# w2's rows 8 to 10 loaded in four DMAs of 112, 6, 6 and 4 partitions

## Chip, cores and metric

The kernel runs on one core of a Trainium2 chip. The metric is the time of one execution in microseconds (us), the median over several runs. A profiled execution adds a trace with the time of every instruction and DMA packet. Engines are named as in the profile: PE is TensorE, PEld its weight load, DVE VectorE, ACT ScalarE, POOL GpSimd, SP SyncE (which issues the loads). A trailing q (SPq, PEldq) means the engine's sequencer.

## The reference

One decode step of a transformer block for two tokens, with modulation computed from a condition `c`. All arrays are float32.

```
mod = silu(c) @ w_mod                    # six vectors of 512 per token
h   = layernorm(x) * (1 + ca) + sa
x   = x + ga * attention(h, k_cache, v_cache, wq, wo)
                                         # 32 query heads, 8 key heads of 128,
                                         # the last 4096 positions of the cache
h   = layernorm(x) * (1 + cb) + sb
x   = x + gb * (silu(h @ w1) @ w2)       # w1 512 x 1792, w2 1792 x 512
```

## The kernel before

Nearly all of the work is loading: the caches' last 4096 positions and the weights are 97.5 MB, and each byte is used once for two tokens.

All loads but the one of `c` go through SP's queue into `slots`, a ring of eight slots of 16 KB in each of the 128 partitions. `stream(n)` (line 70) hands out the next `n` slots. A load into a slot waits until the instructions that read its former contents are done. In the order of issue the queue carries `w_mod`, `x`, `wq`, then per step one K load and one V load of 4 MB (`load_pair`, line 77; eight steps), then `wo` in two loads, `w1` in two, and `w2` in four. Each of these loads covers all 128 partitions; a partition's piece lies in one run in memory. Sixteen DMA engines share each of them.

`load_runs(w, per, lo, hi)` (line 88) loads a weight matrix. It gives partition `p` the rows `p * per + lo` to `p * per + hi - 1`. For `w2` `per` is 14 (`T2`), and the four loads (lines 593 to 598) are rows 0 to 7, 8 to 10, 11 and 12, and 13 of each partition: 2048, 768, 512 and 256 KB, or 16384, 6144, 4096 and 2048 B for each partition.

The attention runs in eight steps: VectorE transposes K (line 367), TensorE forms scores (L380), ScalarE the exponentials, TensorE the weighted V (L454). After it, the tail, in the order of TensorE, which is written out by hand (`inorder`):

- L584, the product with `wo`, and the second layernorm
- L623, the product with `w1`, then VectorE's silu, which gives `uT` (L653)
- L657: w2's rows 0 to 7, each one matmul of 512 columns into `acc_yw`, in two passes each (16 in the profile)
- L667: w2's rows 8 to 10, four matmuls of 128 columns each into `acc_y` (24 in the profile)
- `gather` (line 563): ScalarE copies `acc_yw` in two halves (L567), and TensorE adds it to `acc_y` (L571)
- L682: w2's rows 11 to 13 into `acc_l`, in halves of 64 columns (48 in the profile)
- VectorE L690 to L698: times `gb`, plus `x`; then SP stores the output (L700)

The matmuls of L667 read tile rows through `w2t[tt]`, so each waits for the load that brought row `tt`. The `busy` matmuls (L554) between the stages write a scratch bank that nothing reads.

Of the kernel before, what the change touches and what calls it, by code (L numbers as in the profile page):

```python
# [13 lines left out]
P = 128  # L14
# [9 lines left out]
def adaln_block(  # L24
# [19 lines left out]
    nc = tc.nc  # L44
# [25 lines left out]
    def stream(n=1):  # L70
        i = turn_of[0]
        if n % 2 == 0:
            i += -i % n
        turn_of[0] = i + n
        return slots[:, i % RING : i % RING + n, :].rearrange("p s e -> p (s e)")
# [9 lines left out]
        )  # L85
        return t

    def load_runs(w, per, lo, hi):

        e = w.shape[1]  # L90
        n = -(-(hi - lo) * e // 4096)
        t = stream(n)[:, : (hi - lo) * e].rearrange("p (q e) -> p q e", e=e)
        nc.sync.dma_start(t, w.rearrange("(p q) e -> p q e", q=per)[:, lo:hi, :])
        return t


# [2 lines left out]
    x_sp, c_sp = xc[:, 0, :], xc[:, 1, :]  # L99
    nc.vector.memset(xc, 0.0)  # L100
    wm = load_runs(w_mod, 4, 0, 4)
    rows8 = lambda t: t.rearrange("(ab r) m -> ab r m", r=16)[:, 0, :]
    for b in range(B):
        for lo in (0, 2):
# [3 lines left out]
            )  # L108
    nc.sync.dma_start(rows8(x_sp), x2.rearrange("b (g m) -> g b m", m=P))  # L109
    wqt = load_runs(wq, 4, 0, 4)  # L110


# [157 lines left out]
    for k in range(4):  # L270
        ab = wm[:, k, : 2 * D].rearrange("p (s g m) -> p g s m", s=2, g=4)
        cd = wm[:, k, 2 * D :].rearrange("p (s g m) -> p g s m", s=4, g=4)
        for g in range(4):
            r = slice(32 * g, 32 * g + 32)
            nc.tensor.matmul(m_a[r, :], scT[:, k, :], ab[:, g], start=(k == 0), stop=(k == 3))  # L275
        for g in range(4):
            r = slice(32 * g, 32 * g + 32)
# [230 lines left out]
    for lo, hi in ((0, 24), (24, 32)):  # L508
        wt = load_runs(wo, 32, lo, hi)
        wot.extend(wt[:, q, :] for q in range(hi - lo))  # L510
    xT = turned(x_sp, "xT")
    w1t = []
    for lo, hi in ((0, 3), (3, 4)):
        wt = load_runs(w1, 4, lo, hi)
# [78 lines left out]
    T2, WIDE = F // P, 8  # L593
    w2t = {}
    for lo, hi in ((0, WIDE), (WIDE, 11), (11, 13), (13, T2)):
        wt = load_runs(w2, T2, lo, hi)
        for tt in range(lo, hi):
            w2t[tt] = wt[:, tt - lo, :]
    aoT = once.tile([P, 4, 32], F32, tag="zp", name="aoT")
# [78 lines left out]
    for tt in range(11, T2):  # L678
        for h in range(2):
            for g in range(4):  # L680
                lo = g * P + h * H
# [11 lines left out]
    for h in range(2):  # L693
        r = slice(h * H, (h + 1) * H)
        inorder(nc.vector.tensor_mul(yo[:, r], yl[h], gb[:, r]))
    for h in range(2):
        r = slice(h * H, (h + 1) * H)
# [30 lines left out]
```

## Time and profile before

| what | value |
|---|---|
| median of 3 runs | 236.15 us (235.47 to 236.29) |
| the profiled execution's own time | 235.3 us |
| its span, first to last instruction | 233.6 us |
| loads in it | 97.53 MB, 418 GB/s over the span |
| TensorE matmul busy | 163.9 us, 70% |
| VectorE busy | 115.2 us, 49% |
| mean granted TensorE clock | 0.925 |

How to read the rows that follow: a row of the chain of waits is start, length, and the work that released what comes next. A row of the timeline is start, length, engine, line, operation, output and inputs with their shapes, the number of instructions, and in brackets the idle time before them and what ended it. A row of stretches gives the busy time of PE, PEld, DVE, ACT and POOL with their numbers of instructions, the granted clock, the DMA engines' mean busy share, and GB/s. A DMA answer counts packets and how many of them are small. A packet is counted in the stretch in which it starts, so shares of short stretches scatter around 1.

### The profile page before, as it was taken

How to read it: one execution, taken by the hardware profiler on the slowest of the kernel's cores; microseconds unless marked ns; L12 is line 12 of the kernel's file. 1: busy time of each engine (PE TensorE's matmuls, PEld its weight loads, DVE VectorE, ACT ScalarE, POOL GpSimd, SP SyncE). 2: the span in 40 equal slices, each digit the busy share in tenths (PEclk: the TensorE clock that was granted, in tenths of full speed). 3: DMA queues.
4: the chain of work that ended last, by engine and by line, in shares of the span. 5: the costliest groups of instructions: out<-in, count | busy, mean ns of one | idle time of the engine just before them, and what ended most of it. 6: DMA issues, size and time to landing. Idle time of an engine off the chain costs nothing.

```text
span 233.6 us, 2452 instructions
## 1 busy us (share of the span) xinstructions
PE 163.9 (70%) x998; PEld 41.1 (18%) x998; DVE 115.2 (49%) x180; ACT 33.5 (14%) x90; POOL 10.1 (4%) x34
## 2 busy tenths in 40 slices
PE   0004906959697839797598769748759786799984
PEld 0001401301111111211110201201111122233322
DVE  0007230187894758695197189259559540200332
ACT  2000210000311120130310201111030041000321
POOL 3004610000000000000000000000000000000000
PEclk9999995999859985999979979999997999899999
DMA  7998998999999999999999999999999999989991
GB/s 269 438 551 359 404 494 359 446 445 415 410 432 449 446 443 404 421 438 446 449 438 404 426 431 449 449 421 410 424 449 449 443 424 438 466 356 438 423 409 63
DMA packets 3794, 97.68 MB, mean 418 GB/s; under 512 B 432, under 2 KB 456, under 8 KB 968
## 3 DMA queue, kind: packets, MB, share of 16 engines
q1 hardware_dynamic: 3768, 97.53, 97.2%
q8 instruction: 8, 0.13, 0.2%
q14 instruction: 2, 0.02, 0.0%
q10 hardware_dynamic: 16, 0.00, 0.0%
HBM read 97.53 MB, written 0.00 MB: 418 GB/s over the span
## 4 chain that ended last, share of the span: by engine, by line
DMA 61%; issue 17%; DVE 13%; PE 6%; POOL 0%; SPq 0%; POOLq 0%; ACT 0%; DVEq 0%
DMA slots<-in_A_k_cache_dram 22%; DMA slots<-in_A_wq_dram 15%; DMA slots<-in_B_w_dram 12%; DMA slots<-in_A_v_cache_dram 12%; DVE kT L367 11%; PE q L308 3%; PE o L454 2%; DVE zp L426 1%; PE acc_yw L657 1%; DVE xp L424 1%; PE acc_l L682 0%; PE acc_y L667 0%; DVE qT L321 0%; POOL qg L325 0%; SPq L109 0%
## 5 line engine op out<-in xcount | busy, mean ns | idle before, releaser
L367 DVE STREAM_TRANSPOSE kT<-slots 128x1024 f32<-128x1024 f32 x64 | 73.7, 1211 | 22.7 <-DMA slots<-in_A_k_cache_dram 22.6
L380 PE MATMUL s<-kT,qbd 128*32 128x512 f32 x256 | 68.5, 714 | 17.6 <-DVE kT L367 16.6
L454 PE MATMUL o<-slots,ptb 128*32 128x512 f32 x256 | 29.1, 595 | 1.1 <-DMA slots<-in_A_v_cache_dram 1.1
L380 PEld LDWEIGHTS s<-kT,qbd 128*32 128x32 f32 x256 | 9.8, 115 | 69.1 <-DVE kT L367 65.1
L275 PE MATMUL m_a<-slots,scT 128*32 128x256 f32 x32 | 4.4, 500 | 20.6 <-DVE scT L267 20.6
L308 PE MATMUL q<-slots,hq_T 128*32 128x512 f32 x64 | 9.3, 745 | 7.7 <-DMA slots<-in_A_wq_dram 7.7
L554 PE MATMUL junk<-quad,id 128*32 128x512 f32 x24 | 12.9, 672 | 0.0
L466 ACT ACTIVATE ob<-o,own 128x128 f32<-128x128 f32 x32 | 9.1, 368 | 23.9 <-PE o L454 23.9
L410 ACT COPY bias<-bp 128x1 f32<-128x1 f32 x8 | 1.3, 159 | 75.3 <-PE bp L408 75.3
L454 PEld LDWEIGHTS o<-slots,ptb 128*32 128x32 f32 x256 | 7.7, 109 | 16.3 <-issue 16.2
L390 DVE TENSOR_REDUCE mx<-s 128x1 f32<-128x512 f32 x8 | 5.5, 692 | 9.6 <-PE s L380 9.6
L441 ACT ACTIVATE ptb<-pT,odd 128x256 f32<-128x256 f32 x16 | 6.7, 477 | 23.1 <-PE pT L433 23.1
L474 PE MATMUL o_all<-ob,selh 128*64 128x512 f32 x16 | 8.7, 622 | 2.0 <-ACT ob L466 2.0
L426 DVE TENSOR_TENSOR zp<-xp,quarter 128x1024 f32<-128x1024 f32 x8 | 9.8, 1226 | 0.2
L261 DVE STREAM_TRANSPOSE cT<-xc 128x128 f32<-128x128 f32 x1 | 0.4, 402 | 16.8 <-DMA xc<-in_c_dram 16.8
L321 DVE STREAM_TRANSPOSE qT<-q 128x512 f32<-128x512 f32 x2 | 1.4, 716 | 13.8 <-PE q L308 11.9
L433 PE MATMUL pT<-zp,mix 128*32 128x256 f32 x64 | 5.9, 446 | 2.8 <-DVE zp L426 2.3
L584 PE MATMUL acc_o<-slots,oTn 128*32 128x512 f32 x64 | 7.7, 593 | 0.0
L600 DVE STREAM_TRANSPOSE aoT<-ao 128x128 f32<-128x128 f32 x1 | 0.3, 316 | 14.8 <-PE ao L571 14.8
L392 PE MATMUL mT<-ident,mx 128*1 128x128 f32 x16 | 3.0, 271 | 6.4 <-DVE mx L390 6.4
L424 DVE STREAM_TRANSPOSE xp<-pr 128x512 f32<-128x512 f32 x8 | 5.5, 685 | 3.4 <-ACT pr L412 3.4
L278 PE MATMUL m_sp<-slots,scT 128*32 128x512 f32 x32 | 6.6, 712 | 0.0
(138 smaller groups left out, 90.1 us busy)
## 6 DMA issues: line engine op xcount, KB each, us to landing
slots<-in_A_k_cache_dram SPq DMA_DIRECT2D x8, 4096.0 KB, 27.6
slots<-in_A_v_cache_dram SPq DMA_DIRECT2D x8, 4096.0 KB, 27.8
slots<-in_w_mod_dram SPq DMA_DIRECT2D x1, 6144.0 KB, 17.0
slots<-in_A_wo_dram SPq DMA_DIRECT2D x1, 6144.0 KB
slots<-in_B_w_dram SPq DMA_DIRECT2D x1, 2688.0 KB
slots<-in_A_wo_dram SPq DMA_DIRECT2D x1, 2048.0 KB, 29.5
slots<-in_B_w_dram SPq DMA_DIRECT2D x1, 2048.0 KB
slots<-in_B_w_dram SPq DMA_DIRECT2D x1, 896.0 KB
```

The lines of the kernel that those rows point to most:

```text
L278: nc.tensor.matmul(m_sp[r, :], scT[:, k, :], cd[:, g], start=(k == 0), stop=(k == 3))
L308: nc.tensor.matmul(q_ps[n][32 * g : 32 * g + 32, :], hq_T[:, k, :], wv[:, n, g], start=(k == 0), stop=(k == 3),)
L367: inorder(nc.vector.transpose(kT[s, j][:, 32 * c : 32 * c + 32, :], kt[s].rearrange("p (n j r) -> p j n r", j=4, r=32)[:, j, 32 * c : 32 * ...
L380: inorder(nc.tensor.matmul(s_ps[s][r : r + 32, :], qbd[h // 4][:, h % 4, b, j, :], kT[s, j][:, 32 * c : 32 * c + 32, e:32:2], start=(j == ...
L424: inorder(nc.vector.transpose(xp, pr[s]))
L426: inorder(nc.vector.tensor_mul(zp, xp[:, None, :, 0:16].to_broadcast([P, 4, 16, 16]), quarter[:, :, None, None].to_broadcast([P, 4, 16, 16 ...
L441: inorder(nc.scalar.activation(ptb[s % 2][:, :, e, :], tp.rearrange("p (w z) -> p w z", z=16), AF.Copy, scale=odd[:, e : e + 1],))
L454: inorder(nc.tensor.matmul(o_ps[s][r : r + 32, :], ptb[s % 2][:, w].rearrange("p e z -> p (e z)"), vt[s].rearrange("p (c w m f d) -> p c f ...
L466: inorder(nc.scalar.activation(o_sb[s][:, c], o_ps[s][:, c], AF.Copy, scale=own[:, m : m + 1]))
L474: inorder(nc.tensor.matmul(o_all, selh[:, lo : lo + 2 * HQ], o_sb[s], start=(s == 0), stop=(s == STEPS - 1)))
L554: inorder(nc.tensor.matmul(junk[0:32, :], id4, quad.rearrange("p m y -> p (m y)"), start=True, stop=True,))
L584: inorder(nc.tensor.matmul(acc[32 * g : 32 * g + 32, :], oTn[:, q, :], wot[q], start=(q < 4), stop=(q >= 28),))
```

## The change

`load_runs` gets an argument `parts`, the numbers of partitions of consecutive DMAs, with one DMA of 128 as its default. Only the load of w2's rows 8 to 10 uses it: 112 partitions (0 to 111), then 6 (112 to 117), 6 (118 to 123) and 4 (124 to 127). The bytes, their places in `slots`, and the instructions that read them stay the same. SP issues three DMAs more.

```
-    def load_runs(w, per, lo, hi):
+    def load_runs(w, per, lo, hi, parts=(P,)):
 ...
         t = stream(n)[:, : (hi - lo) * e].rearrange("p (q e) -> p q e", e=e)
-        nc.sync.dma_start(t, w.rearrange("(p q) e -> p q e", q=per)[:, lo:hi, :])
+        src, at = w.rearrange("(p q) e -> p q e", q=per)[:, lo:hi, :], 0
+        for rows in parts:
+            r = slice(at, at + rows)
+            nc.sync.dma_start(t[r], src[r])
+            at += rows
+        assert at == P
         return t
 ...
     for lo, hi in ((0, WIDE), (WIDE, 11), (11, 13), (13, T2)):
-        wt = load_runs(w2, T2, lo, hi)
+        wt = load_runs(w2, T2, lo, hi, (112, 6, 6, 4) if lo == WIDE else (P,))
```

## The prediction

> **What bounds the kernel now.** I read the page first, then the chain of waits, then TensorE's timeline, then the DMA answers in narrow windows, because the edited load is one of the last four and only the tail can change.
>
> ```profile
> span 233.6 us, 2452 instructions
> ...
> DMA packets 3794, 97.68 MB, mean 418 GB/s; under 512 B 432, under 2 KB 456, under 8 KB 968
> ...
> q1 hardware_dynamic: 3768, 97.53, 97.2%
> q8 instruction: 8, 0.13, 0.2%
> ...
> q10 hardware_dynamic: 16, 0.00, 0.0%
> ```
>
> The kernel is a stream: the one queue that carries all loads keeps its 16 DMA engines busy 97.2% of the span. From that row comes the price of a packet: 97.53 MB over 0.972 x 16 x 233.6 us is 26.8 KB per us and engine. A packet is one partition's piece of a load; in the edited load it is 3 rows of 512 floats, 6144 B, so 0.229 us. A load over 128 partitions gives each engine eight of them.
>
> The end of the chain (start, length, what):
>
> ```profile
> 197.16 29.02 DMA slots<-in_B_w_dram
> 226.17 0.14 issue
> 226.31 1.92 PE acc_yw L657 x16
> 228.23 0.78 PE acc_y L667 x24
> 229.01 0.45 PE acc_y L571 x8
> 229.46 0.82 PE acc_l L682 x40
> ...
> 230.79 0.14 DVEq L724
> ```
>
> The chain comes down the w2 loads to 226.17, when rows 0 to 7 have landed, and then seems to be TensorE. The timeline and the source answers say more:
>
> ```profile
> 226.31 1.92 PE L657 MATMUL acc_yw<-slots,uT 128*32 128x512 f32 x16 [0.72 <-DMA slots<-in_B_w_dram]
> 228.15 0.86 PE L667 MATMUL acc_y<-slots,uT 128*32 128x128 f32 x24
> ...
> 229.37 0.98 PE L682 MATMUL acc_l<-slots,uT 128*32 128x64 f32 x48
> ```
> ```profile
> L667 PEldq EVENT_SEMAPHORE  x1: 51/51/51, 228.0 to 228.0; - x1
> ```
> ```profile
> L682 PEldq EVENT_SEMAPHORE  x1: 51/51/51, 229.3 to 229.3; - x1
> ```
> ```profile
> L93 SPq DMA_DIRECT2D slots<-in_B_w_dram x3: 328/328/328, 209.8 to 213.2; - x3
> ...
> DMA to landing us min/median/max: 16.6/16.6/16.6
> ```
>
> TensorE's weight loader stands at a semaphore just before L667 and just before L682, and the last load, issued at 213.2, lands 16.6 us later, at 229.8. L682's 48 matmuls take 0.98 us for three w2 rows, so the last 16 begin near 230.0, about 0.2 after that landing, where the first wait of the tail shows 0.14 from landing to matmul (226.17 to 226.31). So each stage of the tail starts within about 0.1 us of the load it needs. **A later landing of rows 8 to 13 is passed on nearly whole; an earlier one gains little**, because rows 0 to 7, which the edit does not touch, still land at 226.17. Their 16 matmuls then fill TensorE until 228.23, and ScalarE copies their sums for L571:
>
> ```profile
> 228.35 0.65 ACT L567 COPY acc_y_sb<-acc_yw 128x256 f32<-128x256 f32 x2 [3.68 <-PE acc_yw L657]
> ```
>
> The second half of L571 cannot start before 229.0 (228.35 + 0.65), however early the other loads are, so L682 could start near 229.2 at best in place of 229.37: a gain of at most about 0.2.
>
> How evenly the engines finish is the other half. Each engine ends its part of a load with a 4 B packet, so the packets under 512 B are finishing marks. Three windows of the DMA answer, 223.9 to 224.6, 224.6 to 225.05 and 229.05 to 229.6, then the busy time of the engines by stretches (the last two numbers are the DMA share and GB/s):
>
> ```profile
> DMA packets 33, 0.26 MB, mean 375 GB/s; under 512 B 7, under 2 KB 7, under 8 KB 23
> ```
> ```profile
> DMA packets 18, 0.15 MB, mean 337 GB/s; under 512 B 0, under 2 KB 0, under 8 KB 14
> ```
> ```profile
> DMA packets 26, 0.04 MB, mean 71 GB/s; under 512 B 7, under 2 KB 7, under 8 KB 26
> ```
> ```profile
> 223.00:224.00 1.00, 1.00 (x7) 0.22 (x2) 0.86 (x3) 0.00 (x0) 0.00 (x0) 1.00 1.05 449
> ...
> 226.00:227.00 1.00, 0.69 (x8) 0.34 (x12) 0.00 (x0) 0.00 (x0) 0.00 (x0) 1.00 1.05 436
> 227.00:228.00 1.00, 1.00 (x12) 0.16 (x4) 0.00 (x0) 0.00 (x0) 0.00 (x0) 1.00 0.92 371
> 228.00:228.50 0.50, 0.50 (x17) 0.38 (x17) 0.00 (x0) 0.15 (x1) 0.00 (x0) 1.00 0.62 250
> 228.50:229.00 0.50, 0.50 (x24) 0.41 (x15) 0.00 (x0) 0.49 (x2) 0.00 (x0) 1.00 0.50 193
> 229.00:229.50 0.50, 0.50 (x19) 0.31 (x17) 0.00 (x0) 0.00 (x0) 0.00 (x0) 1.00 0.26 98
> ```
>
> Seven engines finish w2's rows 0 to 7 early, none follows for 0.45 us, and nine are late; at the very end the DMA share runs down from 0.62 to 0.26 instead of stopping at once. The engines are uneven by more than a microsecond, and the late ones set every landing.
>
> **The change part by part.**
>
> *How the loads fall on engines.* The count of marks tells how a load spreads: 26 loads over 128 partitions at 16 marks are 416 of the 432. The four loads of c, two rows each, have 16 packets in all (the row of q10), so two data packets and two marks each: two rows on two engines. The remaining 8 marks belong to x and the output, 8 rows each: four engines each. I take 112 rows as 16 engines x 7, and the small loads as one row per engine on the same engines each time: 6, 6 and 4. Then four engines carry 7+1+1+1 = 10 packets, two carry 9 and ten carry 7, where all carried 8. In time: ten engines give up 0.229 us, four gain 0.46, two gain 0.23. If the 16 single rows fell on 16 different engines instead, every engine would have 8 again and nothing would move. The Trainium skill ("DMA: Bandwidth & Descriptors", the section on why a DMA increments its semaphore by 16) says that the lowest-numbered engines are used; no view quoted here numbers the engines.
>
> *What this does to the end if packets keep their price.* The late engines finish 0.23 earlier unless the loaded ones are among them. The four may finish up to 0.69 (three packets) after where they stand against the last before the gain is gone. The gap of the marks says that seven engines have that room. The landing moves by -0.23 to +0.46. TensorE can use at most about 0.2 of a gain, as shown above. This part is -0.2.
>
> *What a packet costs in the new split.* Every packet of the loads before belongs to a load of 128 partitions, eight per engine, and the queue's 97.2% says these engines never got in each other's way. The edit shifts the borders: seven partitions per engine, then single neighbouring partitions on four to six engines at once. No row of the trace has that, so I bound it. From below: no effect, the packet stays at 0.229 (a gain is excluded: the engines already run at this price for 97.2% of the span). From above, for the 112-partition load: each of its seven packets meets another engine's on the way into the same partitions and goes at half rate, 7 x 0.229 = +1.60. For the small loads: four engines on one way, three times, 3 x 3 x 0.229 = +2.06. The rows of before all have the old split, so they lie near neither end, and I take the middle of both: +0.8 and +1.0.
>
> Here a page bears on the row. The Trainium skill ("SBUF — State Buffer", section "Door 1: The DMA port swizzle") has the partitions behind 16 ports, in groups of four with the group 32 further on sharing the port, and "DMA: Bandwidth & Descriptors" ("The descriptor swizzle") has a load of 128 partitions laid out so that each engine writes one port. By these pages the full rate of the row is what that layout buys, and the estimate for the new split is: two of seven packets met by another engine, +0.46, and partitions 112 to 115 behind one port, so 3 x 3 x 0.229 = +2.06, less 0.2: +2.3. By the row alone it would be -0.2. Nothing run so far decides between them.
>
> *Issue.* Three more DMAs are issued by SP, 0.328 us each: +1.0 us on SP's queue, ahead of the loads of rows 11 to 13. The edited load is issued at 209.8 and those loads wait 16.6 us in the queue, so this costs nothing. SP's later wait is the output's, at 230.79. Without the cover it would cost the 1.0. SP may also wait for an earlier DMA before it reuses a semaphore; w1's loads, the latest such, were issued before w2's and are ahead in the same queue.
>
> *TensorE's wait.* L667 waits for four loads where it waited for one: up to three more semaphore steps of 0.051 us, +0.15 at most. Behind it on TensorE stand L667, L571 and L682, and behind those VectorE. I take 0, since three of the four steps pass while the last load is still on its way. The floor is 0, since no step is taken away.
>
> **The sum** against the profiled execution: -0.2 + 0.8 + 1.0 + 0 + 0 = +1.6 us, 235.3 to 236.9. That execution is 0.85 under the median of the runs (236.15) and just under the fastest (235.47), so on the median's footing the time is 236.15 + 1.6 = 237.7 us.
>
> **The rivals.**
>
> *No meeting of engines; not slower.* Packets keep 0.229 us in any split. Place: the landing of rows 8 to 13. It decides when the four loaded engines have at least three packets, 0.69 us, of room against the last one. For it: the steady 97.2% and the seven early marks. Against it: that row holds for one split only. Time: 236.15 - 0.2 = 235.95.
>
> *The loaded engines are late ones.* Packets keep their price but the four with ten packets are among the nine late. Then the end moves by up to 2 x 0.229: 236.6. For it: nine of sixteen are late. Against it: the last marks are spread, so a late engine need not be a last one.
>
> *The small loads do not spread.* x's 8 rows went on four engines, not eight, so a load need not take one engine per row. If six rows went on one engine each time, it would carry 7 + 6 + 6 + 4 = 23 packets, 15 more: +3.4, 239.6. Against it: c's two rows did spread.
>
> *Faster by more than the sum allows.* Fetches of code delay single engines (8 packets on q8); should they fall otherwise, the late group could shrink. Nothing in the edit moves TensorE's code, and 1.2 us would be the whole gap between the groups: 235.0.
>
> **How the numbers follow.** A measurement of this kernel can tell about 0.5%, 1.18 us, from no change. Chances: engines meet, 0.56, of it 0.46 above +1.18 and 0.10 between +0.6 and +1.18; no meeting, 0.31; late engines loaded, 0.06; no spread, 0.04; faster, 0.03. So slower by over 0.5% is 0.46 + 0.04 = 0.50, within it 0.10 + 0.31 + 0.06 = 0.47, faster 0.03. The likeliest case by itself runs from +0.6 to its two upper ends less the gain, 1.60 + 2.06 - 0.2 = +3.46: 236.7 to 239.6. The range for 8 in 10 reaches down past the case without meeting, 235.8, and stops at +3.25, 239.4, leaving out the far end of the first case, the unspread loads and the gain.
>
> **What would show it.** If engines meet: in the DMA answer around 224 to 229 the 6144 B packets are fewer per microsecond with the DMA share still near 1, so GB/s falls well under the 371 to 449 of before; the semaphore step before L667 comes at 229 or later instead of 228.0, and L682's start moves by the same amount, with the end 3.8 us after the last landing as now (229.8 to 233.6). If they do not: L667 starts near 228.0 and L682 near 229.2. Loaded late engines would show a last mark about 0.4 us later at an unchanged rate; unspread loads, fewer than 16 + 6 + 6 + 4 = 32 marks in place of 16, so a total under 448 packets below 512 B. The forecast is wrong if L667 still starts by 228.3.

## The result and the profile after

The changed kernel takes 239.25 us (median of 5 runs, 238.89 to 239.78) where the kernel before takes 235.63 (5 runs, 235.44 to 236.29): a ratio of 1.0147, 95% interval 1.0124 to 1.0170, or +3.5 us (here and below the ratio times the median of before; the medians themselves differ by 3.6). It is slower, as forecast, by a little over twice the forecast 1.6 us, and its time lies just under the upper end of the range, 239.4.

The lines of helpers moved by five: L662 is the old L657, L672 the old L667, L576 the old L571, L687 the old L682, L96 the old L93. The end of the chain of waits of the changed kernel (start, length, what):

```profile
197.54 31.03 DMA slots<-in_B_w_dram
228.57 0.14 issue
228.71 3.20 PE acc_yw L662 x16
231.90 1.18 PE acc_y L672 x24
233.08 0.26 PE acc_y L576 x8
```

The load of rows 0 to 7, which the edit does not touch, lands at 228.57 in place of 226.17. Up to the tail the two profiled executions differ little: SP issues the load of rows 0 to 7 at 197.16 before and at 197.54 after. So 0.38 us of the spans' difference of 3.9 (237.5 against 233.6) lie before the tail, and the rest, 3.5, in it. TensorE's timeline and its semaphore steps:

```profile
228.71 3.20 PE L662 MATMUL acc_yw<-slots,uT 128*32 128x512 f32 x16 [2.79 <-DMA slots<-in_B_w_dram]
231.88 1.20 PE L672 MATMUL acc_y<-slots,uT 128*32 128x128 f32 x24
...
233.11 0.86 PE L687 MATMUL acc_l<-slots,uT 128*32 128x64 f32 x48
```
```profile
L672 PEldq EVENT_SEMAPHORE  x2: 51/51/51, 231.5 to 231.8; - x2
```

The step ahead of L672 comes at 231.8 (228.0 before), and L672 starts right behind it; L687 starts at 233.11 (229.37 before). From L672 on the tail has moved by about 3.7 us, and most of that at the landings: by the packet records of the two traces (start, time and size of each packet) the last data packet of w2 ended at 229.53 before and at 232.90 after, 3.4 later. Where the bytes went is in the stretches, the changed kernel first, then the same stretch of the kernel before (the last two numbers are the DMA share and GB/s, the one ahead of them TensorE's granted clock):

```profile
224.00:226.00 2.00, 1.92 (x5) 0.33 (x3) 1.36 (x7) 0.23 (x1) 0.00 (x0) 1.00 1.06 305
226.00:228.00 2.00, 0.00 (x0) 0.00 (x0) 0.00 (x0) 0.00 (x0) 0.00 (x0) 1.00 0.96 173
228.00:230.00 2.00, 1.29 (x12) 0.47 (x16) 0.00 (x0) 0.00 (x0) 0.00 (x0) 0.80 1.00 184
230.00:232.00 2.00, 2.00 (x16) 0.31 (x12) 0.00 (x0) 0.00 (x1) 0.00 (x0) 0.50 0.77 226
```
```profile
226.00:228.00 2.00, 1.69 (x16) 0.50 (x16) 0.00 (x0) 0.00 (x0) 0.00 (x0) 1.00 0.99 404
```

From 226 to 230 the engines are as busy as ever, 0.96 and 1.00, and move 173 and 184 GB/s, where the kernel before moved 404 while it had work. They are not idle and not short of work; each packet takes longer. In the packet records all 128 packets of rows 8 to 10 took 234 ns before; after, their median is 444 ns and the longest took 754.

### The profile page after: what moved, and what is told of

It reads as the page before. It is cut to its first block, busy times and chain, and to the rows that moved or that the text cites. A ratio compares the mean times of both kernels' runs of the same rounds, so it can differ in the third digit from the quotient of the medians.

```text
span 237.5 us, 2459 instructions
## 1 busy us (share of the span) xinstructions
PE 164.2 (69%) x998; PEld 41.5 (17%) x998; DVE 115.1 (48%) x180; ACT 33.5 (14%) x90; POOL 10.1 (4%) x34
## 4 chain that ended last, share of the span: by engine, by line
DMA 61%; issue 17%; DVE 13%; PE 6%; POOL 0%; SPq 0%; POOLq 0%; ACT 0%; DVEq 0%
DMA slots<-in_A_k_cache_dram 21%; DMA slots<-in_A_wq_dram 15%; DMA slots<-in_B_w_dram 13%; DMA slots<-in_A_v_cache_dram 12%; DVE kT L372 11%; PE q L313 2%; PE o L459 2%; PE acc_yw L662 1%; DVE zp L431 1%; DVE xp L429 1%; PE acc_y L672 0%; DVE qT L326 0%; POOL qg L330 0%; SPq L114 0%; DVE qbd L340 0%
```

## The experiments

The theory is that engines meet: partitions are reached over ways that engines share, and a split which puts two engines on one way slows both. Its rivals: uneven engines (10, 9 and 7 packets), a fixed price for each DMA, and the reading side (the order in which the rows of w2 are read). Each ratio is to the kernel before, run on the same chip.

### Even counts: 112 and 16

```
-        wt = load_runs(w2, T2, lo, hi, (112, 6, 6, 4) if lo == WIDE else (P,))
+        wt = load_runs(w2, T2, lo, hi, (112, 16) if lo == WIDE else (P,))
```

> Rows 8 to 10 in two loads, 112 and 16 partitions, so every engine again has 8 packets of 6144 B. Shared ways (partitions reach memory over ways that several engines can meet on): most of the changed kernel's +3.5 us stays, +1.2 to +3.0 against the kernel before. Uneven engines (the cost is the 10 packets on four engines): within 0.2 us of the kernel before. A fixed price for each DMA (three more cost 3.5): one more costs about +1.2.

Measured: 1.0142 (1.0126 to 1.0158), +3.3 us, within the noise the same as the change itself, and just above the +3.0 that was expected at most. Uneven counts are not the cause, and two DMAs fewer than in the change bring nothing back.

```profile
226.00:228.00 2.00, 0.00 (x0) 0.00 (x0) 0.00 (x0) 0.00 (x0) 0.00 (x0) 1.00 0.91 160
```

The same stretch again shows busy engines (0.91) at 160 GB/s.

### Three loads that keep the split of 128

```
-        nc.sync.dma_start(t, w.rearrange("(p q) e -> p q e", q=per)[:, lo:hi, :])
+        src = w.rearrange("(p q) e -> p q e", q=per)[:, lo:hi, :]
+        ...  # rows 8 to 10 of w2:
+            for q in range(hi - lo):
+                nc.sync.dma_start(t[:, q, :], src[:, q, :])
```

> Rows 8, 9 and 10 in three loads of all 128 partitions, 2048 B each; each engine keeps its 8 partitions. Shared ways: no meeting, -0.2 to +0.2 us. Uneven engines: the same, even by count. A fixed price for each DMA: two more cost about +2.3.

Measured: 1.0016 (0.9998 to 1.0035), +0.4 us at an interval that reaches no change. A fixed price of 1.2 us for each DMA is out.

### Two halves

```
+        wt = load_runs(w2, T2, lo, hi, (64, 64) if lo == WIDE else (P,))
```

> Rows 8 to 10 in two loads of 64 partitions, 4 packets for each engine and load, even by count. Shared ways: if 64 partitions have half of the ways, two engines are on each way all the time, 8 x 0.229 = +1.8 us or more, since the engines that are still at rows 0 to 7 are met too. Uneven engines: 0. A fixed price for each DMA: about +1.2.

Measured: 1.0182 (1.0139 to 1.0225), +4.3 us, with equal counts and one DMA more. Its four runs scatter (238.5 to 240.5), so the interval, +3.3 to +5.3, overlaps that of the change: the halves cost at least about as much. The expected floor of 1.8 holds; the size is about twice that or more. The stretches of its profiled execution, one of the two shorter runs:

```profile
226.00:228.00 2.00, 0.00 (x0) 0.00 (x0) 0.00 (x0) 0.00 (x0) 0.00 (x0) 1.00 1.01 238
228.00:230.00 2.00, 1.60 (x16) 0.50 (x16) 0.00 (x0) 0.00 (x0) 0.00 (x0) 1.00 1.04 240
```

### The small loads by themselves

```
         nc.sync.dma_start(t, src)
+        ...  # behind rows 8 to 10 of w2, into the unused rest of their slot:
+            for rows in (6, 6, 4):
+                nc.sync.dma_start(spare[at : at + rows], src[at : at + rows])
+                at += rows
```

> The kernel before, and behind its load of rows 8 to 10 three further loads of 6, 6 and 4 partitions (112 to 127) into a part of the slot that nothing reads; L667 does not wait for them. It is the small loads by themselves, without the 112. Shared ways: 16 packets behind four engines' ways, between 4 x 0.229 = 0.9 more for these ways and 2.7 for the four engines that do three each, less their room: +0.5 to +2.5 us. Uneven engines: at most three packets for four engines, 0.69, less their room: 0 to +0.5. A fixed price for each DMA: +3.5.

Measured: 1.0061 (1.0046 to 1.0076), +1.4 us, within what meeting engines were expected to cost and above what uneven counts could.

### The same split on more and on fewer bytes

```
+        wt = load_runs(w2, T2, lo, hi, (112, 6, 6, 4) if lo == 13 else (P,))   # first kernel
+        wt = load_runs(w2, T2, lo, hi, (112, 6, 6, 4) if lo == 0 else (P,))    # second kernel
```

> The split 112, 6, 6, 4 on the load of row 13 alone, 2048 B for each partition in place of 6144. Shared ways: the price goes with the bytes, a third of +3.5: about +1.2 us. A fixed price for each DMA: +3.5.

> The split 112, 6, 6, 4 on the load of rows 0 to 7, 16384 B for each partition, 8/3 of the bytes. Shared ways: 8/3 of +3.5, about +9 us. A fixed price for each DMA: +3.5.

Measured: 1.0030 (1.0017 to 1.0044), +0.7 us, on row 13; 1.0433 (1.0414 to 1.0452), +10.2 us, on rows 0 to 7. With 1/3, 1 and 8/3 of the bytes the price is 0.7, 3.5 and 10.2: it grows with the bytes, and a fixed price is out again. How closely it follows them is shown for the two larger loads alone. In the profiled execution of the row 13 kernel the chain of waits from 195 us to the end is computation, with no load on it, and the packets of w2 took only 0.1 us more for each engine, so +0.7 is not the price of its loads there. In the kernel with rows 0 to 7 the low rate begins earlier and lasts longer. Two of its stretches:

```profile
222.00:224.00 2.00, 2.00 (x23) 0.76 (x19) 0.17 (x1) 0.77 (x2) 0.00 (x0) 1.00 1.03 238
228.00:230.00 2.00, 0.00 (x0) 0.00 (x0) 0.00 (x0) 0.00 (x0) 0.00 (x0) 1.00 0.89 119
```

### Sixteen neighbours, or every eighth partition: not conclusive

```
+        wt = load_runs(w2, T2, lo, hi, (16,) * 8 if lo == WIDE else (P,))      # both kernels
+            to = t[r] if rows != 16 else t[at // 16 :: 8]                      # second kernel
```

> Rows 8 to 10 in eight loads of 16 neighbouring partitions, one packet for each engine and load, even by count. Shared ways, in groups of four neighbours: four engines on each way all the time, 8 x 3 x 0.229 = +5.5 us. Reading side (the cost comes from the order in which rows are read): whatever it is, the same as in the kernel with spread destinations. Uneven engines: 0. A fixed price for each DMA: seven more, +8.

> The same eight loads reading the same rows in the same order, but each writes every eighth partition, so w2's rows 8 to 10 land in other partitions and the output is another one. Shared ways: at most two engines on each way, 8 x 0.229 = +1.8 us, clearly under the kernel with neighbouring partitions. Reading side, or a fixed price for each DMA: the same as that kernel.

Measured: 1.0120 (1.0100 to 1.0140) and 1.0132 (1.0109 to 1.0156), +2.8 and +3.1 us: no difference, where meeting engines were expected to give 5.5 and 1.8. Taken alone this speaks for the reading side. But eight loads brought a wait of another kind. SP's waits and the stretches of the kernel with neighbours:

```profile
SPq L96 <- DMA slots<-in_B_w_dram: 13.5, 3, 6.2
```
```profile
226.00:228.00 2.00, 1.48 (x4) 0.22 (x2) 0.97 (x5) 0.23 (x1) 0.00 (x0) 1.00 0.52 141
228.00:229.00 1.00, 0.83 (x8) 0.34 (x12) 0.00 (x0) 0.00 (x0) 0.00 (x0) 1.00 0.31 117
```

SP waited three times, 13.5 us in all, for earlier loads of w1 and w2 before it issued the next, and the engines stood at 0.52 and 0.31. Why a load is held for an earlier one was not tried by itself. Both kernels measure this wait as well, so the next kernels add four loads only.

### The deciding trio: same reads, other partitions

Each is the kernel before with four more loads of 8 rows (32 packets) into the unused rest of the slot. All three read the same rows in the same order; only the partitions that they write differ.

```
+            for i in range(4):
+                nc.sync.dma_start(spare[i : i + 29 : 4], src[8 * i : 8 * i + 8])            # own
+                nc.sync.dma_start(spare[8 * i : 8 * i + 8], src[8 * i : 8 * i + 8])         # near
+                nc.sync.dma_start(spare[64 + i : 64 + i + 29 : 4], src[8 * i : 8 * i + 8])  # other
```

> The kernel before, and behind its load of rows 8 to 10 four further loads of 8 rows each into a part of the slot that nothing reads: partitions 0, 4, 8 to 28, then the same moved up by 1, 2 and 3. By the Trainium skill (SBUF, Door 1; DMA, The descriptor swizzle) each of the first eight engines then writes its own port. Shared ways by these pages: every 6144 B packet keeps its price; eight engines carry four packets more, 0.92 us, less their room: +0.3 to +0.9 us. Reading side: as the kernel with neighbouring partitions.

> The same four loads, the same rows read by the same engines and the same 32 partitions written in the end, but each load writes eight neighbours: 0 to 7, 8 to 15, 16 to 23, 24 to 31. Shared ways by these pages: four engines meet on a port in each load, 0.92 + 4 x 3 x 0.229 = up to +3.7 us, at the least 1 us more than the spread ones, with many slow packets. Reading side, or a fixed price for each DMA: the same as the spread ones, within 0.3 us.

> The same four loads spread over partitions 64 to 95, which by these pages are ports that the other eight engines write. Shared ways: two engines on a port while both stream, +0.9 to +1.8 us, with slow packets also in the loads of rows 11 to 13. Reading side: the same as the spread ones on partitions 0 to 31.

Measured: 1.0032 (1.0019 to 1.0044), +0.75 us; 1.0086 (1.0066 to 1.0105), +2.0; 1.0104 (1.0087 to 1.0120), +2.5. The stretches, one fence for each kernel in that order:

```profile
226.00:228.00 2.00, 2.00 (x12) 0.47 (x14) 0.91 (x5) 0.23 (x1) 0.00 (x0) 1.00 1.00 413
```
```profile
226.00:228.00 2.00, 1.80 (x17) 0.50 (x16) 0.09 (x1) 0.00 (x0) 0.00 (x0) 1.00 1.05 331
```
```profile
226.00:228.00 2.00, 2.00 (x12) 0.51 (x14) 0.95 (x5) 0.23 (x1) 0.00 (x0) 1.00 1.04 268
```

With the reads alike, the same bytes cost 1.3 us more when each load writes eight neighbours than when it writes every fourth partition, and 1.7 more when the spread ones lie 64 partitions further on. The rates say the same: 413, 331 and 268 GB/s at full shares. So do the packet records: of the 160 packets of 6144 B, none, 42 and 62 took over 1.3 times their 234 ns. SP's waits do not make the difference, since all three issue their last load alike, at 221.5 to 221.7. The reading side is out: the price is on the writing side and depends on which partitions are written. Partitions 64 to 95 cost more than expected (+0.9 to +1.8).

The first kernel's +0.75 is not all a price of its loads. In its profiled execution TensorE's granted clock fell to 0.60 from 194 to 198 us, where the kernel before has 1.00:

```profile
194.00:198.00 4.00, 4.00 (x28) 1.39 (x24) 0.00 (x0) 0.00 (x0) 0.00 (x0) 0.60 0.94 406
```

From there to the end the chain of waits is computation, and no load of w2 is on it. The last data packet of w2 ended at 230.46, 0.9 us later than before.

### Halves again, as even and odd partitions

```
+            to = t[r] if rows != 64 else t[at // 64 :: 2]
 ...
+        wt = load_runs(w2, T2, lo, hi, (64, 64) if lo == WIDE else (P,))
```

> Two loads of 64 partitions as in the kernel with halves, the same rows read, but written to the even and then the odd partitions; rows land in other partitions, so the output is another one. Shared ways by these pages: each load now reaches all 16 ports in place of 8, so the hard doubling is gone and only passing meetings are left: +0 to +1.8 us, clearly under the halves' +4.1. Reading side: the same as the halves.

Measured: 1.0015 (1.0002 to 1.0027), +0.35 us, against +4.3 for the halves. Two loads of 64 partitions, the same rows read; only the destinations differ.

```profile
226.00:228.00 2.00, 2.00 (x9) 0.38 (x10) 1.22 (x6) 0.23 (x1) 0.00 (x0) 1.00 1.00 410
```

410 GB/s is the rate of the kernel before (404), and all 128 packets of rows 8 to 10 took 234 ns again. The 0.35 left is not on them: here too the chain from 195 us to the end is computation. No load is cheaper for being whole; what matters is how its partitions fall on the ways.

## Why the prediction was right, and where it was not

**The mechanism held.** The likeliest case was that engines meet on the way into the partitions. Its signs were named and came: GB/s far under the rate of before at a share near 1 (173 and 184), the semaphore step ahead of L672 at 229 or later (231.8), L687 moved by the same amount (3.7). A later landing was passed on nearly whole, as taken. The trio and the even and odd halves show that the destination alone makes the difference.

**The spread of the small loads** was as taken: 448 finishing marks, the 16 + 6 + 6 + 4 in place of 16.

```profile
DMA packets 3810, 97.68 MB, mean 411 GB/s; under 512 B 448, under 2 KB 472, under 8 KB 984
```

**The step that failed** is that the price of meeting was put on the split load's own packets alone, with rows 0 to 7 that "still land at 226.17" and rows 11 to 13 at their old price. But an engine that is met is slowed too. The packet records show where the time went. The packets' extra time, summed and divided by 16 engines, is 1.78 us on the split load and 1.48 on loads that the edit does not touch: 0.45 on rows 0 to 7, 0.85 on rows 11 and 12, and 0.18 on row 13. Seven engines leave rows 0 to 7 by 224.4, as before, and begin with the split load; of the 16 KB packets that others start after that, some took up to 1501 ns, where each took 611 before. So the landing of rows 0 to 7 moved by 2.4 us (0.38 of it from before the tail). The halves show the same: 1.31 on their own packets and 1.51 on the others. With partitions 64 to 95 rows 11 and 12 paid 0.75, and rows 0 to 7 nothing. The upper end of the bounds, 1.60 + 2.06 - 0.2 = +3.46, was met by another sum than the one it stood for.

**The two prices**, +0.8 for the 112 partitions and +1.0 for the small loads, were middles between bounds. Their sum, 1.8, is what the split load's own packets paid, and that is partly luck: 1.78 is an average over 16 engines, and +1.0 was meant for four. The trace does not tell the 112 from the small loads. By themselves the small loads measured +1.4, their 16 further packets included, and 112 with 16 measured +3.3, so the terms hold at most for the split load's own packets, and not for what the split costs.

**A reading that does not hold** is that the queue's 97.2% says that the engines never got in each other's way. In the changed kernel the share is as high, 0.96 and 1.00, while they do. What says it for the kernel before is that its packets all keep one price, 234 ns for each of rows 8 to 10.

**What the engines' room was worth** cannot be seen: the gain of 0.23 us for the late engines lies under a loss fifteen times its size. In the kernel with four packets more on eight engines the last data packet came 0.9 us later, so four packets of 0.23 us were paid about in full.

**The other terms.** SP's three DMAs more delayed its queue by far more than the 1.0 us of the forecast. The last load was issued at 219.5 in place of 213.2, since SP first waited 5.9 us for an earlier load of w1 or w2, as the prediction said it might:

```profile
L96 SPq DMA_DIRECT2D slots<-in_B_w_dram x6: 278/332/352, 210.1 to 219.5; - x6
```
```profile
SPq L96 <- DMA slots<-in_B_w_dram: 5.9, 1, 5.9
```

It stayed hidden all the same: rows 0 to 7, ahead of that load in the queue, landed at 228.57. TensorE's waits: two steps in place of one ahead of L672, of which one came at 231.5, before the last landing, so at most one step of 0.05 us is on the path.

**The ports.** The Trainium skill ("SBUF — State Buffer", "Door 1: The DMA port swizzle") has 16 ports, with groups of four neighbouring partitions on a port, and 64 to 95 on others than 0 to 31. The Trainium skill ("DMA: Bandwidth & Descriptors", "The descriptor swizzle") has each engine write one port in a load of 128 partitions. The trio agrees with both: 413 GB/s for the partitions that this layout gives the first eight engines as their own, 331 for eight neighbours, 268 for the other engines' ports. The estimate made from the Trainium skill ahead of the run, +2.3, came nearer than the forecast's +1.6, and fell short for the same reason: it counted only the split load's packets.

**What stays open.** No view numbers the engines, so which engines met, and how the 112 fall on them, was not seen. Two engines at half rate do not explain all of it: 754 ns for a packet of 234, or 1501 for one of 611, is more than double. Whether more than two met there, or a meeting costs more than the sharing, was not settled.

## What to carry to other kernels

Before splitting a load by partitions, ask which partitions each engine will write: a load of 128 partitions, or its even and odd halves, left the stream at about 404 to 410 GB/s here (226 to 228 us), while 64 neighbours, 112 + 16, or small runs of neighbours took it to 160 to 331. A busy share near 1 with falling GB/s is the sign of it; the share alone shows nothing. And bound such a price by all loads that are in flight beside the edited one, not by its own bytes.

## What the runs showed of the hardware

Two things that were not expected. The price spreads to loads that were not changed, as told above. And TensorE's clock fell when its work went on after the long wait for w2: the granted clock is 1.00 up to 228, then 0.80 and 0.50 in the two stretches to 232. A matmul of L662 took 1038 ns (median); its 16 together took 3.20 us, where the old L657's took 1.92:

```profile
L662 PE MATMUL acc_yw<-slots,uT x16: 589/1038/1061, 228.7 to 230.8; 128*32 128x512 f32 x16
```

In the changed kernel this lies mostly beside the wait for rows 8 to 10, which landed after these matmuls' last start. In the halves' profile TensorE waits about as long, and the granted clock is 1.00 in the stretches shown. Its span is 237.2 against 237.5, so the clock is not the cause of the loss, and why it fell in one and not in the other is not shown.
